# A folded, two-step DFT with a hand-given PE order, in place of a three-level DFT with PE transposes

## Chip, cores, metric

One core of one Trainium2 chip. The metric is the device time of one execution, in microseconds (us), lower is better. A run is called slow here when it took over 1.5% longer than the fastest run of the same kernel. PE is the matmul engine, DVE the vector engine, ACT the scalar engine, POOL the GpSimd engine, SP the sync engine, which in these kernels only issues DMAs.

## The reference, cut

A GFNet block followed by a token MLP, forward and backward in one program: S = 2048 tokens, D = 448, F = 1792, bf16.

```python
def _A_ref(x, w_r, w_i):                        # spectral filter
    X = rfft2(x.astype(f32), axes=(-2, -1))     # 2048 x 225 complex
    return irfft2(X * (w_r + 1j * w_i), s=(S, D)).astype(bf16)
def _B_ref(x, w1, b1, w2, b2):                  # MLP over tokens
    u = gelu(einsum("bsd,sf->bdf", _layernorm(x), w1) + b1)
    return (einsum("bdf,fs->bds", u, w2) + b2).transpose(0, 2, 1)
h  = x + _A_ref(_layernorm(x), w_r, w_i)
h2 = h + _B_ref(_layernorm(h), w1, b1, w2, b2)
# outputs: h2 and the gradients of x, w_r, w_i, w1, b1, w2, b2 for a given grad_out
```

Names used below: `u` = w1ᵀ·LN(h), `y` = w2ᵀ·g, `dg` = w2·grad_out, `dh` = w1·du; gw1, gw2 are the weight gradients (out_4, out_6); the gradients of w_r and w_i are out_2 and out_3; W is w_r and w_i together.

## The kernel before

Every transpose is done on PE (a matmul with the identity) and evicted from PSUM. The DFT over tokens is done in three levels, with one pair of 256-wide matmuls for each of 29 blocks of 8 columns. W is loaded across all 128 partitions. DMAs go out alternately on the ACT and POOL queues; SP is idle.

```python
dma_engs = [nc.scalar, nc.gpsimd]
...
def rfft2(src, dst, before_c=None):
    for t in range(NT):                                   # DFT over columns
        for j in range(4):
            nc.tensor.transpose(tp[:, j, :], src[:, t, DBASE[j]:DBASE[j] + P], ident[:])
        evac(out=xt[:], in_=tp[:])
        for j in range(4):
            nc.tensor.matmul(pa[:], lhsT=xt[:, j, :], rhs=fd[:, j, :, :], ...)
        ...
    for kb in range(NKB):                                 # 29 blocks
        for c in range(2):
            nc.tensor.transpose(tps[:, c, :], at[:, c, kb, :, :], ident[:])
        evac(out=tt[:], in_=tps[:])
        nc.tensor.matmul(pb[:], lhsT=tt[:, 0, :], rhs=kA[:], start=True, stop=False)
        nc.tensor.matmul(pb[:], lhsT=tt[:, 1, :], rhs=kB[:], start=False, stop=True)
        ...
...
dma(w_b[:, :, 0, 0:DF], A_w_r.rearrange("(q r) k -> q r k", r=NR))      # W: 128 partitions
...
def w2T_blocks(j):                                        # w2 transposed on PE for dg
    for tg in range(0, NT, 4):
        pt, _ = transpose_blocks(None, [w2t[:, j, t * P:(t + 1) * P] for t in range(tg, tg + 4)], None, "tr")
        evac(out=blk[:, tg:tg + 4, :], in_=pt[:])
```

The stages run one after the other: forward spectral, u, gw2, y, dg, gw1, dh, backward spectral.

## Time and profile before

584.12 us median of 3 runs (583.54 to 585.63). Lines of the page: busy time of PE; PE's busy share in 40 equal slices of the span, in tenths; the same for the DMA engines (mean of 16); packets; and per DMA queue its packets, megabytes, and the time that its packets took as a share of 16 engines over the span.

```profile
span 582.7 us, 8976 instructions
...
PE 472.2 (81%) x3364; PEld 281.9 (48%) x3364; DVE 360.2 (62%) x912; ACT 301.6 (52%) x640; POOL 47.1 (8%) x94
...
PE   0287687979997999999999989997999989487600
...
DMA  9030155359702333211660423331000470001124
...
DMA packets 25555, 65.53 MB, mean 112 GB/s; under 512 B 8376, under 2 KB 13560, under 8 KB 24872
...
q0 software_dynamic: 8176, 34.50, 15.6%
q10 hardware_dynamic: 17336, 30.47, 15.0%
...
```

PE is busy 472.2 of 582.7 us, so 110.5 us are idle: some 51 of them at the two ends and 49 in the two spectral stretches (windows below). The DMA queues together take 31% of the 16 engines: there is room.

The windows view gives, for a stretch of time, the busy us and instruction count of each engine, the granted PE clock, the DMA share and the GB/s:

```profile
...
core 0: us, PE busy (x) PEld busy (x) DVE busy (x) ACT busy (x) POOL busy (x), PEclk, DMA share, GB/s
0.00:28.00 28.00, 2.40 (x18) 1.67 (x18) 21.96 (x94) 8.71 (x21) 4.79 (x26) 1.00 0.48 132
28.00:129.00 101.00, 79.33 (x680) 54.81 (x681) 83.46 (x208) 70.06 (x133) 10.45 (x15) 0.97 0.34 129
...
236.00:279.00 43.00, 43.00 (x236) 22.52 (x235) 10.65 (x16) 0.76 (x2) 4.34 (x8) 1.00 0.14 53
...
458.00:558.00 100.00, 73.09 (x592) 47.85 (x590) 79.66 (x181) 62.37 (x167) 6.36 (x11) 0.91 0.22 73
558.00:583.00 25.00, 0.00 (x0) 0.00 (x0) 13.39 (x24) 0.00 (x0) 3.02 (x4) 0.50 0.40 81
...
```

236–279 (a part of the MLP) is pure PE. In the spectral stretches 28–129 and 458–558 PE is busy 79 and 73 us of about 100 and DVE 80 to 83. The ends, 0–28 and 558–583, hold 2.4 us of PE work together.

Groups of instructions (count, busy us, mean ns of one, then the engine's idle time before them and who ended it):

```profile
...
L658 ACT COPY w2T<-ps_tr 128x512 bf16<-128x512 bf16 x33 | 17.4, 592 | 73.9 <-PE ps_tr L547 52.4
L715 PE MATMUL ps_mm<-du_t,hlt 128*128 128x512 bf16 (+1 forms) x256 | 49.5, 353 | 0.3
...
L668 PE MATMUL ps_mm<-xn,w2T 128*128 128x448 bf16 x224 | 44.7, 352 | 0.0
...
L220 PE MATMUL ps_tr<-ident,cinv 128*128 128x128 bf16 x16 | 2.1, 310 | 23.4 <-ACT cinv L213 23.4
...
```

The MLP matmuls (L715, L668) wait for nothing. The w2 transposes are evicted by ACT, in pieces of 0.59 us (L658), and by DVE; PE starts only when a table is there (L220, 23.4 us).

### The profile page before, as it was taken

The page shows a single profiled execution, that of the slowest core. Times are in us where ns is not written, and L with a number is a line of the kernel's source. Part 1 is how long each engine was busy: PE and PEld are TensorE (multiplying, and loading weights), DVE is VectorE, ACT ScalarE, POOL GpSimd, SP SyncE. Part 2 cuts the span into 40 slices and gives each one's busy share as a digit, 9 for nine tenths or more (in the row PEclk, how much of TensorE's full clock was granted, in tenths as well). Part 3 has the DMA queues.
Part 4 walks back from the last instruction along what each step waited for, and adds up shares of the span by engine and source line. Part 5 has one row for each costly group of instructions (what it writes and reads, how often), then busy time and mean ns, then how long its engine had stood idle before and what let it go on. Part 6 is the DMA issues. An engine that isn't in the chain of part 4 may idle for free.

```text
span 582.7 us, 8976 instructions
## 1 busy us (share of the span) xinstructions
PE 472.2 (81%) x3364; PEld 281.9 (48%) x3364; DVE 360.2 (62%) x912; ACT 301.6 (52%) x640; POOL 47.1 (8%) x94
## 2 busy tenths in 40 slices
PE   0287687979997999999999989997999989487600
PEld 0144475544546444555666555554666557364200
DVE  5988687795779721122444343322777857967983
ACT  0569776546997655100144164443666347378800
POOL 3000013021000000110300100000000100001111
PEclk9999899999997999999999999998999999699855
DMA  9030155359702333211660423331000470001124
GB/s 253 1 127 36 74 207 190 134 181 394 274 1 112 131 158 145 96 43 46 257 265 2 164 90 144 139 127 65 0 1 2 167 219 1 0 2 33 63 85 74
DMA packets 25555, 65.53 MB, mean 112 GB/s; under 512 B 8376, under 2 KB 13560, under 8 KB 24872
## 3 DMA queue, kind: packets, MB, share of 16 engines
q0 software_dynamic: 8176, 34.50, 15.6%
q10 hardware_dynamic: 17336, 30.47, 15.0%
q8 instruction: 26, 0.43, 0.3%
q14 instruction: 17, 0.14, 0.1%
HBM read 36.27 MB, written 28.69 MB: 111 GB/s over the span
## 4 chain that ended last, share of the span: by engine, by line
PE 59%; DVE 20%; ACT 13%; issue 5%; DMA 3%; ACTq 0%; DVEq 0%
PE ps_mm L627 8%; PE ps_mm L715 8%; PE ps_mm L668 7%; PE ps_mm L636 7%; PE ps_mm L739 7%; PE ps_tr L547 5%; PE ps_mm L345 4%; PE ps_mm L393 2%; PE ps_mm L357 2%; DVE stats_h L435 1%; ACT uf L567 1%; DVE hn L523 1%; DVE gx L818 1%; DVE ln_stats L435 1%; PE ps_mm L394 1%
## 5 line engine op out<-in xcount | busy, mean ns | idle before, releaser
L658 ACT COPY w2T<-ps_tr 128x512 bf16<-128x512 bf16 x33 | 17.4, 592 | 73.9 <-PE ps_tr L547 52.4
L715 PE MATMUL ps_mm<-du_t,hlt 128*128 128x512 bf16 (+1 forms) x256 | 49.5, 353 | 0.3
L627 PE MATMUL ps_mm<-goT,g_t 128*128 128x512 bf16 x224 | 49.3, 379 | 0.0
L564 PE MATMUL ps_mm<-hln,w1c 128*128 128x448 bf16 x224 | 44.6, 362 | 3.8 <-DVE hln L442 3.8
L739 PE MATMUL ps_mm<-gp,w1T 128*128 128x448 bf16 x224 | 46.3, 361 | 0.3 <-issue 0.3
L668 PE MATMUL ps_mm<-xn,w2T 128*128 128x448 bf16 x224 | 44.7, 352 | 0.0
L636 PE MATMUL ps_mm<-gT,w2t 128*128 128x448 bf16 x224 | 42.5, 352 | 0.0
L715 PEld LDWEIGHTS <-hlt 128*128 128x128 bf16 x256 | 24.6, 98 | 24.4 <-ACT hlt L709 1.2
L564 PEld LDWEIGHTS <-w1c 128*128 128x128 bf16 x224 | 22.4, 100 | 25.8 <-issue 6.6
L627 PEld LDWEIGHTS <-g_t 128*128 128x128 bf16 x224 | 21.7, 98 | 25.3
L636 PEld LDWEIGHTS <-w2t 128*128 128x128 bf16 x224 | 21.9, 98 | 20.5
L739 PEld LDWEIGHTS <-w1T 128*128 128x128 bf16 x224 | 21.7, 100 | 19.3 <-issue 2.3
L345 PE MATMUL ps_mm<-fd,xt 128*128 128x464 bf16 x128 | 27.5, 365 | 3.8 <-DVE xt L342 3.5
L668 PEld LDWEIGHTS <-w2T 128*128 128x128 bf16 x224 | 21.4, 98 | 18.0
L670 DVE TENSOR_TENSOR gp<-ps_mm,gp 128x448 bf16<-128x448 f32 x14 | 8.7, 625 | 31.3 <-PE ps_mm L668 31.3
L357 PE MATMUL ps_mm<-kA,tt 128*128 128x256 bf16 x58 | 15.2, 278 | 7.8 <-DVE tt L355 4.5
L220 PE MATMUL ps_tr<-ident,cinv 128*128 128x128 bf16 x16 | 2.1, 310 | 23.4 <-ACT cinv L213 23.4
L743 ACT ACTIVATE junk<-ps_mm 128x448 bf16<-128x448 f32 x16 | 8.7, 544 | 22.6 <-PE ps_mm L739 22.6
L381 ACT CAST vt_t<-ps_mm 128x464 bf16<-128x464 f32 x26 | 13.1, 577 | 13.8 <-issue 8.5
L345 PEld LDWEIGHTS <-xt 128*128 128x128 bf16 x128 | 11.7, 99 | 16.4 <-DVE xt L342 4.5
L729 ACT COPY w1T<-ps_tr 128x512 bf16<-128x512 bf16 (+1 forms) x32 | 16.8, 582 | 3.0 <-DMA out_dram<-st_4501 2.9
L547 PE MATMUL ps_tr<-ident,w1n 128*128 128x128 bf16 x224 | 15.3, 219 | 3.2 <-DVE w1T L729 3.2
(676 smaller groups left out, 1112.2 us busy)
## 6 DMA issues: line engine op xcount, KB each, us to landing
w1c<-in_B_w_dram POOLq DMA_DIRECT2D x7, 1024.0 KB, 10.0
w2t<-in_B_w_dram ACTq DMA_DIRECT2D x7, 512.0 KB, 15.7
w2t<-in_B_w_dram POOLq DMA_DIRECT2D x7, 512.0 KB, 10.6
w1n<-in_B_w_dram ACTq DMA_DIRECT2D x8, 448.0 KB, 15.9
w1n<-in_B_w_dram POOLq DMA_DIRECT2D x8, 448.0 KB, 9.0
xspec_d<-xspec POOLq DMA_DIRECT2D x1, 1856.0 KB, 6.0
xspec_b<-xspec_d POOLq DMA_DIRECT2D x1, 1856.0 KB, 11.9
xln_d<-xln ACTq DMA_DIRECT2D x1, 1792.0 KB
```

The source lines that it names most:

```text
L345: nc.tensor.matmul(pa[:], lhsT=xt[:, j, :], rhs=fd[:, j, :, :], start=(j == 0), stop=(j == 3))
L357: nc.tensor.matmul(pb[:], lhsT=tt[:, 0, :], rhs=kA[:], start=True, stop=False)
L381: evac(out=vt[:, :, :, r, :], in_=pv[:, :, :].rearrange("p c (kb k) -> p c kb k", k=8))
L547: nc.tensor.transpose(pt[:, i, :], src_blocks[i], ident[:])
L564: nc.tensor.matmul(pu[:], lhsT=w1c[:, t, jj * P:(jj + 1) * P], rhs=hln[:, t, :], start=(t == 0), stop=(t == NT - 1))
L627: nc.tensor.matmul(pw[:], lhsT=g_t[:, jj, j * P:(j + 1) * P], rhs=goT[:, jj, ch * 512:(ch + 1) * 512], start=(jj == 0), stop=(jj == 3))
L636: nc.tensor.matmul(py2[:], lhsT=w2t[:, j, t * P:(t + 1) * P], rhs=gT[:, j, :], start=(j == 0), stop=(j == NFB - 1))
L658: evac(out=blk[:, tg:tg + 4, :], in_=pt[:])
L668: nc.tensor.matmul(pdg[:], lhsT=cur[:, t, :], rhs=go[:, t, :], start=(t == 0), stop=(t == NT - 1))
L715: nc.tensor.matmul(pw[:, 0:cw], lhsT=hlt[:, jj, :], rhs=du_t[:, jj, ch * 512:ch * 512 + cw], start=(jj == 0), stop=(jj == 3))
L729: evac(out=blk[:, jg:jg + n, :], in_=pt[:, 0:n, :])
L739: nc.tensor.matmul(pdh[:], lhsT=cur[:, j, :], rhs=duT[:, j, :], start=(j == 0), stop=(j == NFB - 1))
```

## The change

Intent: fewer and larger matmuls for the DFT, no transposes on PE, and no idle PE in the spectral stages, by putting matmuls of dg, gw2 and gw1 between their steps.

- The rows are folded (x[k] ± x[-k]), so the column DFT needs half the products; the token DFT has two steps, with a scatter through SBUF-to-SBUF DMAs between them.
- All transposes become DMA transposes on the SP queue.
- `fill(n)` puts n pending MLP matmuls into the PE order at given places; the other engines' orders are worked out by a timeline simulation when the kernel is built.
- In the new spectral layout, W loads and stores come in 18 pieces of 16 partitions each, on the POOL queue.

```diff
+N_FILL_F = (50, 4, 16, 3, 16, 2)
+N_FILL_B = (16, 16, 60, 9, 16, 12)
...
-        for tg in range(0, NT, 4):
-            pt, _ = transpose_blocks(None, [w2t[:, j, t * P:(t + 1) * P] for t in range(tg, tg + 4)], None, "tr")
-            evac(out=blk[:, tg:tg + 4, :], in_=pt[:])
+    def load_w2T(j):
+        wT = w2T_ring.next()
+        nc.sync.dma_start_transpose(out=wT, in_=B_w2[j * P:(j + 1) * P, :].rearrange("f (t c) -> f t c", c=P))
+        return wT
...
-    dma(w_t[:, :, 0, 0:DF], A_w_r.rearrange("(q r) k -> q r k", r=NR))
+    def w_io(Wv, dr, di, store, eng):
+            for f in range(4):
+                go((16 * f, 16 * f + 16), 0, 16,
+                   d.rearrange("(a r) k -> a r k", r=P)[:, 16 * f:16 * f + 16, :])
+            for f in range(4):
+                ...                                  # the mirrored half, again 16 partitions each
...
+    def fold_prep(src, t2):
+        ...
+        nc.sync.dma_start_transpose(out=xT, in_=ft.rearrange("p s b c -> p (s b) c"))
+    def d_stage(xT, i):                              # column DFT, then s1_stage and its scatter
+    def s1_stage(s1, ab):
+        ...
+        nc.sync.dma_start(out=D2[s1:P:16, :, 0:2, :], in_=cs)
...
+    pending.append(dg_gen())
+    w_io(W_view_F, A_w_r, A_w_i, False, gp_)
+    fill(N_FILL_F[0])                                # 50 dg matmuls ahead of the first d_stage
+    for s1 in range(NT):
+        nab = d_stage(xTs[s1 // 2], s1 % 2)
+        if s1 >= 1:
+            s1_stage(s1 - 1, ab)
+        fill(N_FILL_F[1])
...
+    nc.sync.dma_start_transpose(out=du_t.rearrange("p j b q -> p (j b) q"), in_=rD[:, 0:NFB * 4 * P])
+    w_io(W_view_B, A_w_r, A_w_i, False, gp_)
+    pending.append(gw2_gen())                        # each block of g and LN(h) through a DMA transpose
+    pending.append(gw1_gen())
+    fill(N_FILL_B[0])
...
```

## The prediction

> **What bounds it now.** The page's busy table gives PE 472 of 582.7 us, 3364 matmuls. By stage (the windows view), the three token-MLP stretches run PE-bound (190 to 334 us is nearly all PE), but the spectral ones do not: 0–28 us has 2.4 us of PE (tables; PE's largest wait is 23 us on the table `cinv`), 28–129 and 458–558 have 79 and 73 us of PE in about 100 each, with DVE at about 80%, and 558–583 has none. Spectral work with start and tail is thus about 255 us; the MLP 330, of which 30 are PE transposes of w1 and w2.
>
> **Removed.** All PE transposes and their PSUM evictions (0.59 us on ACT, 0.42 on DVE for 128x512); the three-level DFT with 29 blocks per direction (256-wide matmuls, evictions of 0.37–0.42 us); the large table chain (2048-wide ACT steps at 2 us); the serial weight-gradient tail.
>
> **Kept.** 1376 MLP matmuls. In the chain of waits 224 of width 448 take 42.4 us (189 ns each), 215 of width 512 take 46.4 (216 ns). Estimate: 266 us.
>
> **Added.** A folded DFT, per direction 64 matmuls of width 226, 80 of 452, 64 of 128, 64 of 448: at 0.1, 0.2, 0.1, 0.2 us (weight loads are 98 ns) about 42 us, so 83 for both. PE falls from 472 to about 350 (1920 matmuls).
>
> **Moved.** dg = w2ᵀ·go (224 matmuls) now fills the forward spectral stages; both weight gradients (480 matmuls, 96 us) fill the backward ones. All transposes go to DMA on the one SP queue: w2 and w1 (7.3 MB each), the folded rows, g, hln, du, go: about 26 MB. [...], mostly hidden.
>
> **Sum (estimate).** PE start at 12–15 us; forward spectral with dg 42+45 plus 15 of latency and table waits → 115; u 46, y 44; dh with six d-pairs 52; backward 96+35 → about 390; tail 8. Stalls that I expect: w1 and w2 column loads (1 MB took 10 us to land, and there are only two buffers against 6.4 us of matmuls): 10–15; w1ᵀ transposes, 448 KB per 2.8 us of PE: 10; the 1.8 MB du transpose ahead of others on SP: 10; ACT in the backward stage (120 evictions of 0.59 plus spectral ones, near 100% of it): 10. About 445 us, PE about 80% busy again.
>
> **Predicted: 445 us, 80% range 405 to 500. Faster by over 2%: 0.97; within 2%: 0.02; slower: 0.01.**
>
> **What would show it.** PE busy 345–380 us, about 1920 matmuls; no transposes on PE; PE starting before 16 us; forward spectral plus dg ending near 115 us; backward spectral plus both gradients about 140 us with PE over 85%; no long stretch without PE at the end (under 12 us); PE's remaining waits naming DMA-fed tiles (rE, r3, r2, rS) and ACT evictions, not DVE.
>
> **What would make it wrong.** DMA transposes much slower than 200 GB/s, or a head-of-line block on SP, where a transpose waits for its buffer ahead of a spectral scatter: then dg, dh or the start of the backward stage stretch by tens of us, towards 500 or more. A granted clock below the 0.945 of now[...].

The sum came to about 390 us, a tail of 8 and 40 to 45 of stalls, about 445; transposes stand in the sum only as 20 us of stalls (w1ᵀ 10, du 10). The 0.1 and 0.2 us for a matmul of the folded DFT are estimates, beside 189 and 216 ns for widths 448 and 512 and 98 ns for a weight load in the kernel before; the 200 GB/s no run had shown.

## The result

552.80 us median of 4 runs (546.42 to 558.94) against 584.64 (583.54 to 585.63) of the kernel before on the same chip: ratio 0.938, 95% interval 0.934 to 0.943, so 6% faster; correct. Predicted were 445 us, 405 to 500. A ratio is the mean time of one kernel's fast runs over that of the other's of the same rounds, so not quite the ratio of the medians that are quoted. The profile below is of the 558.94 us run, a slow one; the fast runs took 546.42 and 550.49.

```profile
span 556.8 us, 6068 instructions
...
PE 386.8 (69%) x1920; PEld 192.2 (35%) x1920; DVE 259.5 (47%) x710; ACT 232.8 (42%) x477; POOL 119.1 (21%) x177
...
PE   0135287485739888986779999935449998399990
...
DMA  9999979759956665259963999799995798986552
...
DMA packets 137344, 87.89 MB, mean 158 GB/s; under 512 B 111136, under 2 KB 127584, under 8 KB 137184
...
q1 hardware_dynamic: 125248, 43.41, 48.2%
q0 software_dynamic: 11488, 42.26, 33.4%
...
```

PE's work fell by 85 us (472.2 to 386.8, 3364 matmuls to 1920), but its idle time rose from 110 to 170 us. The DMA row went from 2 nines in 40 slices to 19: the queues now take 83% of the 16 engines, not 31%. Packets went from 25,555 to 137,344, of which 111,136 are under 512 bytes; q1 is SP's queue, with all transposes; q0 is POOL's.

Windows of after: the start; dg's first 50 matmuls; u; y; dh; and the start of the backward stage.

```profile
...
0.00:25.00 25.00, 0.00 (x0) 0.00 (x0) 16.01 (x60) 2.86 (x3) 14.19 (x29) 1.00 1.00 173
25.00:66.00 41.00, 15.97 (x50) 6.21 (x51) 14.98 (x79) 9.19 (x14) 8.99 (x17) 0.68 1.25 104
...
187.00:237.00 50.00, 43.42 (x227) 21.63 (x225) 34.54 (x90) 23.78 (x32) 6.33 (x6) 1.00 0.49 159
237.00:304.00 67.00, 51.52 (x229) 24.19 (x228) 19.23 (x39) 12.60 (x34) 15.35 (x22) 0.87 0.77 167
304.00:356.00 52.00, 50.21 (x284) 27.33 (x283) 38.99 (x114) 20.44 (x57) 1.08 (x2) 1.00 0.94 176
356.00:420.00 64.00, 32.14 (x122) 13.57 (x120) 5.06 (x15) 17.83 (x34) 13.32 (x25) 0.72 1.12 129
...
```

u and dh went about as planned (50 and 52 us against 46 and 52, clock 1.00). In 0–66 us PE did 16 us of work, with the DMA engines at 1.00 and 1.25 of their time for 173 and 104 GB/s; in 356–420 it did 32 us of 64, DMA at 1.12 for 129 GB/s. (A share over 1 says that records of packets of one engine overlap; I read it as "full".)

```profile
...
L567 PE MATMUL ps_mm<-rC,rE 128*128 128x448 bf16 x224 | 62.9, 418 | 50.0 <-DMA rE<-in_B_w_dram 50.0
L865 PE MATMUL ps_mm<-rG,rst 112*128 112x512 bf16 x224 | 59.7, 418 | 23.4 <-DMA rst<-rE 12.9
L732 PE MATMUL ps_mm<-rE,rS 128*128 128x448 bf16 x224 | 51.0, 396 | 15.5 <-DMA rS<-in_B_w_dram 15.5
...
L809 PE MATMUL ps_mm<-rD,r_73 128*128 128x448 bf16 x224 | 43.5, 353 | 0.6 <-DMA r_73<-in_B_w_dram 0.6
...
```

dg waits 50.0 us for transposed w2 (rE), 25.3 of them at the start; gw2 waits 23.4 for transposed g and for its store buffers, y 15.5 for its w2 columns (rS). dh, fed by w1 transposes of nearly the same size, waits only 0.6: in its stage POOL's queue moves 0.12 MB, against 8.96 on SP's (lines under all_plain), so almost nothing runs beside them. What SP did in the first 64 us (start, us, line, tile, count):

```profile
...
0.75 37.80 SPq L187 DMA_TRANSPOSE rE<-in_B_w_dram  x3
38.67 8.90 SPq L437 DMA_TRANSPOSE rT<-rF  x2
...
```

Three w2 transposes of 512 KB held SP for 37.8 us; the first transposes of folded rows (L437), which the spectral stage needs, stand behind them.

### The profile page after: what moved, and what is told of

Read it like the earlier page. It is cut to its first block, busy times and chain, and to the rows that moved or that the text cites. A ratio compares the mean times of both kernels' runs of the same rounds, so it can differ in the third digit from the quotient of the medians.

```text
span 556.8 us, 6068 instructions
## 1 busy us (share of the span) xinstructions
PE 386.8 (69%) x1920; PEld 192.2 (35%) x1920; DVE 259.5 (47%) x710; ACT 232.8 (42%) x477; POOL 119.1 (21%) x177
## 2 busy tenths in 40 slices
DMA packets 137344, 87.89 MB, mean 158 GB/s; under 512 B 111136, under 2 KB 127584, under 8 KB 137184
## 3 DMA queue, kind: packets, MB, share of 16 engines
q1 hardware_dynamic: 125248, 43.41, 48.2%
q0 software_dynamic: 11488, 42.26, 33.4%
## 4 chain that ended last, share of the span: by engine, by line
DMA 41%; PE 21%; issue 14%; DVE 10%; POOL 7%; ACT 4%; SPq 2%; DVEq 0%; POOLq 0%; ACTq 0%
PE ps_mm L809 6%; PE ps_mm L732 5%; DMA rS<-in_B_w_dram 5%; DMA out_dram<-r_81 4%; DMA rG<-in_A_w_r_dram 4%; DMA r_72<-in_B_w_dram 4%; DMA rD<-in_A_w_i_dram 4%; DMA r_73<-r_78 3%; DMA rE<-in_B_w_dram 3%; DMA rC<-rD 3%; PE ps_mm L880 3%; PE ps_mm L865 2%; DMA xspec_d<-rS 2%; DMA rD<-in_A_w_r_dram 2%; DMA out_dram<-rO 2%
## 5 line engine op out<-in xcount | busy, mean ns | idle before, releaser
L567 PE MATMUL ps_mm<-rC,rE 128*128 128x448 bf16 x224 | 62.9, 418 | 50.0 <-DMA rE<-in_B_w_dram 50.0
L865 PE MATMUL ps_mm<-rG,rst 112*128 112x512 bf16 x224 | 59.7, 418 | 23.4 <-DMA rst<-rE 12.9
L732 PE MATMUL ps_mm<-rE,rS 128*128 128x448 bf16 x224 | 51.0, 396 | 15.5 <-DMA rS<-in_B_w_dram 15.5
L880 PE MATMUL ps_mm<-rC,rst 112*128 112x512 bf16 (+1 forms) x256 | 54.9, 363 | 3.3 <-ACT rO L883 2.0
L567 PEld LDWEIGHTS <-rE 128*128 128x128 bf16 x224 | 24.5, 113 | 78.5 <-DMA rE<-in_B_w_dram 51.6
L687 PE MATMUL ps_mm<-rB,r_72 128*128 128x448 bf16 x224 | 43.5, 353 | 6.6 <-DMA r_72<-in_B_w_dram 4.4
L809 PE MATMUL ps_mm<-rD,r_73 128*128 128x448 bf16 x224 | 43.5, 353 | 0.6 <-DMA r_73<-in_B_w_dram 0.6
L868 ACT CAST rO<-ps_mm 128x512 bf16<-128x512 f32 x54 | 30.4, 598 | 29.7 <-DMA out_dram<-rO 20.5
L865 PEld LDWEIGHTS <-rst 112*128 112x128 bf16 x224 | 23.6, 106 | 55.0 <-issue 20.9
L880 PEld LDWEIGHTS <-rst 112*128 112x128 bf16 x256 | 24.8, 100 | 26.2 <-issue 4.1
L528 PE MATMUL ps_ff<-csI,rAT 113*128 113x448 bf16 x128 | 31.2, 369 | 0.8 <-ACT rAT L517 0.5
L687 PEld LDWEIGHTS <-r_72 128*128 128x128 bf16 x224 | 21.6, 98 | 28.3 <-DMA r_72<-in_B_w_dram 5.9
L517 ACT CAST rAT<-ps_ff 113x512 bf16<-113x512 f32 x32 | 18.6, 589 | 30.2 <-PE ps_ff L514 30.2
L739 DVE SCALAR_TENSOR_TENSOR r_81<-ps_mm,b2col,r_81 128x448 bf16<-128x448 f32 x16 | 10.6, 681 | 43.9 <-DMA r_81<-h_d 37.3
L744 ACT ACTIVATE r_81<-rC 128x448 bf16<-128x448 bf16 x16 | 9.2, 576 | 51.9 <-DVE r_81 L739 38.9
L450 ACT CAST r_78<-ps_ff 128x452 bf16<-128x452 f32 x32 | 17.1, 539 | 30.7 <-PE ps_ff L447 30.5
L809 PEld LDWEIGHTS <-r_73 128*128 128x128 bf16 x224 | 21.7, 97 | 22.9 <-issue 1.8
L463 DVE TENSOR_SCALAR r_72<-r_72 128x904 bf16<-128x904 bf16 x8 | 2.7, 391 | 48.5 <-DMA r_72<-r_78 48.5
```

The costliest lines, as they stand in the source:

```text
L450: sc.copy(out=ab, in_=pv)
L517: sc.copy(out=aT[0:KC].rearrange("p a b -> p (a b)"), in_=pa[0:KC, :])
L528: nc.tensor.matmul(py[:, 0:D], lhsT=aT[0:KC, i, :], rhs=csI[0:KC, i // 2, i % 2, :], start=(i == 0), stop=(i == 3))
L567: nc.tensor.matmul(pg[:, 0:D], lhsT=wT[:, t, :], rhs=go_tp[:, t, :], start=(t == 0), stop=(t == NT - 1))
L687: nc.tensor.matmul(pu[:, 0:D], lhsT=w1c[:, t, jj * P:(jj + 1) * P], rhs=hln[:, t, :, :], start=(t == 0), stop=(t == NT - 1))
L732: nc.tensor.matmul(py[:, 0:D], lhsT=w2cs[t // 2][:, j, (t % 2) * P:(t % 2 + 1) * P], rhs=g_[:, j, :, :], start=(j == 0), stop=(j == NFB - 1))
```

## The experiments

18 kernels ran, in five calls; the kernel before ran beside each call, at 584.9 to 587.0 us, so the chips agree within 0.4%. The changed kernel itself was not run again on those chips, so a gain over it is worked out from the two ratios to the kernel before, (0.938 - ratio) x 585 us, where both have a ratio. (w_wide_split's 0.895 matches the mean of its three runs of 522 to 528 over the kernel before's, not its one fast run of 513.) The four runs of the changed kernel, 546 to 559, show no gap between fast and slow. Kernels with the same, or nearly the same, forward direction ended it at 180.6 to 189.6 us (changed kernel, stores_on_act, y_queue, w_reload, stores_held), so less than 10 us there says nothing. The profiles of the changed kernel, w_wide, stores_on_act, staged_yfree, order_late, combined_staged and best_try are of slow runs; the changed kernel's took 8 to 13 us longer than its fast ones, so stage differences against it can hold that much more than the ratios give. "Wrong" marks a kernel that gives wrong results. The stages, in us, from PE's timeline in each profiled run ("rest" is everything after dh; sums are the span):

| kernel | median | ratio to before | first d stage at | forward end | u | y | dh | rest |
|---|---|---|---|---|---|---|---|---|
| predicted, before 40–45 of stalls | 445 | 0.762 | – | 115 | 46 | 44 | 52 | 139 |
| changed kernel | 552.8 | 0.938 | 66.4 | 187.2 | 50.0 | 66.3 | 52.2 | 201.1 |
| w_wide (wrong) | 515.9 | (one fast run) | 49.0 | 161.3 | 51.3 | 67.0 | 51.7 | 186.5 |
| w_wide_split (wrong) | 523.0 | 0.895 | 43.9 | 165.1 | 49.9 | 67.8 | 52.8 | 175.7 |
| w2_plain (wrong) | 529.2 | 0.901 | 35.3 | 156.9 | 51.7 | 71.0 | 53.0 | 197.2 |
| stores_on_act | 563.6 | (one fast run) | 63.6 | 180.6 | 49.8 | 67.2 | 53.0 | 211.6 |
| all_plain (wrong) | 505.4 | 0.863 | 31.1 | 157.3 | 48.9 | 61.2 | 51.4 | 185.7 |
| w_late | 561.3 | 0.958 | 40.1 | 188.2 | 51.4 | 72.0 | 53.3 | 198.7 |
| y_queue | 558.2 | 0.952 | 65.6 | 182.6 | 49.8 | 77.8 | 52.4 | 193.5 |
| w_reload | 530.3 | 0.908 | 64.0 | 180.7 | 51.6 | 70.6 | 53.2 | 176.9 |
| w_staged | 542.2 | 0.924 | 53.8 | 171.5 | 48.0 | 70.9 | 53.3 | 197.2 |
| staged_plain (wrong) | 488.3 | 0.833 | 30.7 | 148.5 | 50.5 | 60.0 | 51.4 | 174.3 |
| y_free | 549.5 | (two fast runs) | 62.1 | 187.6 | 48.5 | 58.0 | 53.3 | 199.4 |
| staged_yfree | 539.8 | 0.910 | 58.0 | 185.9 | 50.3 | 63.2 | 53.4 | 191.7 |
| order_late | 561.0 | 0.948 | 47.9 | 189.8 | 51.5 | 68.9 | 53.5 | 197.7 |
| stores_held | 543.4 | 0.921 | 71.5 | 189.6 | 51.2 | 67.1 | 53.1 | 181.0 |
| combined | 542.6 | 0.923 | 47.3 | 198.5 | 46.6 | 57.2 | 53.3 | 181.5 |
| combined_staged | 537.9 | 0.909 | 38.5 | 183.8 | 46.1 | 61.6 | 52.7 | 193.4 |
| folds_first | 538.1 | 0.920 | 28.1 | 163.3 | 49.8 | 71.2 | 52.1 | 199.1 |
| best_try | 513.5 | 0.870 | 26.6 | 186.1 | 47.1 | 56.7 | 51.9 | 172.2 |

### Narrow W transfers: w_wide, w_wide_split

Theory N: a transfer to 16 partitions takes long and slows what runs beside it. The rivals are that the transposes alone make the start slow (w_wide) and the number of DMAs (w_wide_split). In the changed kernel's trace the forward pieces of 112.5 KB took 19.9 us (w_r) and 11.4 us (w_i) to land (medians of seven), waits included: a piece of 7.0 KB took 12.7.

```diff
-    w_io(W_view_F, A_w_r, A_w_i, False, gp_)      # and the same for W_view_B
+    for c_, d in ((0, A_w_r), (1, A_w_i)):         # wrong order of rows, same bytes
+        gp_.dma_start(out=W_view_F[:, :, c_, 0:DF], in_=d.rearrange("(q r) k -> q r k", r=NG))
```

> The spectral weights are loaded 128 partitions wide, two transfers for each direction, in place of 18 narrow ones of 16 partitions each (same bytes and the same 450-byte pieces; rows in the wrong order, so the result is wrong on purpose). Theory N (narrow W loads hog the 16 DMA engines while others wait): the first dg group of PE starts before 20 us instead of 25, the 50-matmul fill ends near 45 instead of 66, the stall of PE between 378 and 418 us of the old trace shrinks by 20 to 25, total 495 to 510 us. Rival T (the DMA transposes themselves are too slow at the start): the fill still ends after 58 us, total above 525.

515.89 us (507.80 to 519.57), wrong. The queue lines of its page:

```profile
...
q1 hardware_dynamic: 125248, 43.41, 47.3%
q0 software_dynamic: 10720, 42.25, 30.2%
...
```

POOL's queue (q0) moved the same 42.25 MB in 30.2% of 517.8 us = 156 us of all engines, against 33.4% of 556.8 = 186 in the changed kernel: 30 us less. SP's queue, on which nothing changed, took 245 us (47.3%), not 268: so the time of a packet seems to contain waiting for other traffic, and one stream's saving shows on both. Its one fast run, 507.8, stands against 546.4 and 550.5 of the changed kernel. The d stage starts 17 us earlier, the forward direction ends 26 us earlier, the rest is 15 shorter: theory N in the main. The start itself did not move (first dg group at 27.8, was 25.4), which N had not said: the first w2 transposes are slow for another reason.

w_wide_split loads the same bytes, as wide, in 16 DMAs for each of w_r and w_i:

```diff
+    [... in_=d.rearrange("(q r) k -> q r k", r=NG)[:, g:g + 1, :] for g in range(NG)]   # one DMA per g
```

> The same bytes in 16 transfers per weight, each 128 partitions wide and one row per partition (wrong order again). If it is the narrowness of the destination that costs: as w_wide, 495 to 515 us. If it is the number of transfers (each some 0.5 us of issue on POOL and its fixed time): close to after, 535 to 552.

(In the changed kernel POOL took 0.51 to 0.60 us to issue one narrow forward W load. As for time that does not shrink with the size, its stores of 3.5, 4.0 and 7.0 KB took 2.4, 1.7 and 1.8 us to land, those of 512 KB 5.6.)

522.98 us (513.23 to 528.21), ratio to before 0.895 (0.889 to 0.901). 32 DMAs per direction, against 18 narrow ones, and still 25 us faster than the changed kernel (0.938 - 0.895); its one fast run, 513.2, is 33 to 37 under the changed kernel's. So the count is not what costs; narrowness remains. One more thing differs: the second half of the narrow pieces reads its rows backwards. In the changed kernel's forward direction the four plain pieces of w_r took 21.4 us to land (median) and the mirrored ones 14 to 20, so that is not what makes them slow; the wide pieces of w_wide_split, half as large, took 5.0. What in a narrow piece takes the time, no run shows.

### Transposes: w2_plain, all_plain

```diff
-        nc.sync.dma_start_transpose(out=wT, in_=B_w2[j * P:(j + 1) * P, :].rearrange("f (t c) -> f t c", c=P))
+        nc.sync.dma_start(out=wT, in_=B_w2[j * P:(j + 1) * P, :].rearrange("f (t c) -> f t c", c=P))   # wrong
```

> The 14 blocks of w2 for dg are loaded by plain copies instead of DMA transposes (wrong values on purpose); the narrow W loads stay. Theory T: the first three blocks land in under 20 us, the fill of 50 matmuls ends before 40 us, forward part ends 30 to 40 us earlier, total 510 to 520. Theory N: the fill still waits on W traffic and ends at 50 or later; total 535 or more.

529.15 us (524.31 to 531.62), ratio 0.901 (0.895 to 0.907). The first dg group starts at 10.3 us, not 25.4, the d stage at 35.3. The forward end comes 30 us earlier, as theory T has it, but the total, 22 us less by the ratios, lies between the two theories: y did not gain (71.0, was 66.3).

all_plain does the same to every large transpose (w2, w1, folded rows, g, LN(h), du, grad_out):

> All DMA transposes of weights, rows, g, hln and du become plain copies of about the same bytes (result wrong on purpose; W loads stay narrow). Theory T (the transposes' small packets fill the DMA engines, which everything shares): the page's packet count falls by more than half, backward loses 40 us or more, time 460 to 500. Rival C (what costs is only the order of the one SP queue, or the low granted clock, not the work of a transpose): bytes and order are the same, so the time stays within 3% of after's 546, over 530.

505.40 us (502.67 to 506.30), ratio 0.863 (0.860 to 0.867), 44 us under the changed kernel: theory T, rival C falls. Packets and queues on its page:

```profile
...
DMA packets 41984, 87.88 MB, mean 174 GB/s; under 512 B 5408, under 2 KB 25696, under 8 KB 41696
...
q1 hardware_dynamic: 29888, 43.40, 32.4%
q0 software_dynamic: 11488, 42.26, 31.0%
...
```

And the first line of SP's timeline (start, us):

```profile
...
0.75 1.34 SPq L187 DMA_DIRECT2D rE<-in_B_w_dram  x3
...
```

Same bytes and same order on q1, but the packets took 32.4% of 504.5 us = 163 us of all 16 engines, against 48.2% of 556.8 = 268. So with transposes the queue's packets take 105 us of full DMA time more. Not all of it is work: POOL's queue, on which nothing changed, also fell, from 186 to 156 us (31.0%). And the three w2 blocks that held SP for 37.8 us leave it in 1.34. The dh stage shows the cost of the transposes with almost nothing beside them. The DMA view of 304:356 us in the changed kernel, then of 267:319 in all_plain:

```profile
...
q1 hardware_dynamic: 32472, 8.96, 92.5%
q0 software_dynamic: 80, 0.12, 0.7%
...
q1 hardware_dynamic: 4248, 8.96, 56.8%
q0 software_dynamic: 128, 0.23, 1.3%
...
```

The same 8.96 MB (13 blocks of w1 and 7 of folded rows, and some scatters that are plain in both) took 48.1 us of all 16 engines with transposes and 29.5 as copies: 186 GB/s against 303. So part of the cost is the transposes' own. In this stage it is still hidden: dh takes 52.2 and 51.4 us.

The expected loss of 40 us in the backward stage was wrong: "rest" is 15 shorter, the forward end 30 earlier, y 5 shorter.

### Both together: w_staged, staged_plain

w_staged is a correct way to widen W: a permutation from DRAM to DRAM, then a load (or, for out_2 and out_3, a store) of 128 partitions.

```diff
+            go(wd[0:64, c_, :, :].rearrange("(f a) g k -> f a (g k)", a=16), bass.AP(d.tensor, d.offset, [[16 * DF, 4], [P * DF, 16], [1, 16 * DF]]))
+            ...                                                    # mirrored half, as before but into DRAM
+            eng.dma_start(out=Wv[:, :, c_, 0:DF], in_=wd[:, c_, :, :])
```

> Correct result. All narrow W transfers (forward load, backward load, and the stores of out_2 and out_3) become a permutation from DRAM to DRAM and a load or store that spans 128 partitions. Theory N (16-partition transfers are what is dear): as with the wide wrong loads, d stage at 44 to 52 us instead of 66, the gap from dh to the first backward s2 near 50 us, and the wait at the backward scatter shrinks with the narrow stores gone; time 500 to 520. Rival: what is dear is the 450-byte piece, not the narrowness; then the permutation costs the same again on the DMA engines, and the time stays at 540 or more.

542.17 us (540.70 to 549.07), ratio 0.924 (0.921 to 0.927). Between the two theories: the d stage starts at 53.8 (13 earlier), the gap from dh to the first backward s2 step shrank from 66 to 45 us as expected, but the wait at the backward scatter rose from 9.4 to 16.0 us, where out_2 and out_3 are now moved twice (a likely cause; stores_held below bears on it). By the ratios 8 us were gained.

staged_plain is w_staged with plain copies for transposes (wrong):

> Wrong result on purpose: w_staged with every large transpose a plain copy of the same bytes. If narrow W transfers and transposes together are what the prediction left out, this falls to 455 to 475, near the 445 predicted with nearly free DMA; if a third thing matters as much (granted clock, head-of-line order), it stays over 485.

488.27 us (486.51 to 490.56), ratio 0.833 (0.830 to 0.836), over the 455 to 475 that would have closed the case. By the ratios the miss is (0.938 - 0.762) x 585 = 103 us; the two DMA costs give back 61 of them, and 42 are left. The stage table shows where: forward 148.5 against 115, y 60.0 against 44, rest 174.3 against 139. In its first 150 us PE waits 12.0 us for grad_out, 18.7 in all for ACT's evictions and sign flips of the spectral chain, 6.5 for the scatter, 6.0 for w2 blocks, 5.0 for a table.

### Order of queues: stores_on_act, y_queue, y_free

stores_on_act moves the out_6 and out_4 stores from POOL to ACT.

```diff
-                            gp_.dma_start(out=out_6[j * P:(j + 1) * P, :], in_=o)      # and out_4
+                            sc.dma_start(out=out_6[j * P:(j + 1) * P, :], in_=o)
```

> The stores of both weight gradients are issued from ACT instead of POOL, so that they no longer queue behind the 18 W loads of the backward pass. Theory Q (head-of-line block on the POOL queue is what stops PE between 382 and 418 us): those waits, on the store buffers, fall from about 20 us to under 8, total 530 to 537. Theory N: the W loads saturate the DMA engines anyway and the s2 stage still waits for W or for scatters; under 8 us gained.

563.61 us (554.82 to 563.98), one fast run: no gain, rest 10 us longer. The wait moved from store buffers (10.5) to the transposes of g (12.9 to 23.2). Issued from ACT, the stores gained nothing: the 10.5 us of one wait became 10.3 more of the other. Which DMA engine ran what, this run does not show.

y_queue moves the h_d reads and the out_5 store to ACT:

```diff
-        nc.sync.dma_start(out=ht, in_=h_d[t * P:(t + 1) * P, :])
+        sc.dma_start(out=ht, in_=h_d[t * P:(t + 1) * P, :])
-    gp_.dma_start(out=out_5.rearrange("(j p) -> j p", p=P), in_=gb1r[0:NFB, :])
+    sc.dma_start(out=out_5.rearrange("(j p) -> j p", p=P), in_=gb1r[0:NFB, :])
```

> Correct result. The h_d reads and the out_5 store leave the SP and POOL queues for the ACT queue, in the y stage only. Theory Q-y (the y stage's 15 us over plan are a head-of-line block: h_d reads stand behind the grad_out transposes on SP, w2 loads behind out_5 on POOL): y falls from 66 us to 48 to 55, time down 8 to 15. Rival B (the DMA engines are full in y): y stays at 62 or more and the time within 5 us.

558.24 us (554.78 to 567.55); y is longer, 77.8: this form of the theory falls. POOL's waits in the y stage:

```profile
...
POOL out_dram L740 <- DVE r L739: 42.0, 9, 14.6
POOL rS L666 <- PE ps_mm L732: 33.0, 4, 19.9
...
```

POOL still stood 42 us before out_0 stores (L740) that wait for DVE, and the w2 column loads (L666) came behind them. So y_free moves those stores to ACT too, and takes the bias-gradient step out of the buffer ring:

```diff
-        junk = m448.next()
-        sc.activation(out=junk, in_=go_pt[:, t, :], func=ACT.Copy, accum_out=gb2[:, t:t + 1])
+        sc.activation(out=go_pt[:, t, :], in_=go_pt[:, t, :], func=ACT.Copy, accum_out=gb2[:, t:t + 1])
-        gp_.dma_start(out=out_0[0, t * P:(t + 1) * P, :], in_=h2)          # h_d and out_5 as in y_queue
+        sc.dma_start(out=out_0[0, t * P:(t + 1) * P, :], in_=h2)
```

> Correct result. In the y stage, stores and reloads of h go to the ACT queue, so that the POOL queue holds nothing but the w2 column loads, and the bias-gradient step no longer takes a buffer of the ring that the reloads need. Theory Q2 (w2 column loads stand behind stores that wait for DVE): y falls from 66 to 50 to 55 us, PE's wait on rS under 5 us, time down about 10. Rival B (the loads land late since the DMA engines are full): y over 60.

549.54 us (541.68 to 551.26). y falls to 58.0 (kernels that leave y alone and keep the transposes: 66.3 to 72.0; the five with this edit: 56.7 to 63.2), and POOL now waits only for PE to free its two buffers:

```profile
...
POOL rS L666 <- PE ps_mm L732: 51.8, 6, 19.6
```

So a part of the y stage's excess was a head-of-line block; but PE's wait for w2 columns fell only from 15.5 to 11.1 us, not under 5, and y stays over the 50 to 55 expected. The total hardly moved, and the forward row stage (from its first L528 matmul to u) shows why: it took 31.6 us instead of 22.1. Without a ring buffer to wait for, all sixteen bias-gradient steps (L744) moved up in ACT's order, between the evictions (L517) that the row stage waits for. ACT's timeline of best_try, which has the same edit:

```profile
...
169.80 0.56 ACT L744 ACTIVATE rC<-rC 128x448 bf16<-128x448 bf16 x1
...
170.91 0.56 ACT L744 ACTIVATE rC<-rC 128x448 bf16<-128x448 bf16 x1
...
171.47 0.57 ACT L517 CAST rAT<-ps_ff 113x512 bf16<-113x512 f32 x1
...
```

Each costs ACT about 0.56 us; in 154–187 us ACT is busy 24.0 us in y_free and 14.3 in the changed kernel. The 8 us gained in y were lost one stage earlier, in all five kernels with this edit (row stages of 30 to 32 us, 21 to 22 in all others). That is read from the traces; no run moved the bias steps alone. staged_yfree is this on top of w_staged:

> Correct result. w_staged and y_free together. If their gains add: 490 to 512, under both given kernels. If y_free only moves the wait: within 2% of w_staged.

539.80 us (530.93 to 546.27), ratio 0.910 (0.904 to 0.916), within 2% of w_staged.

### Where the backward stage loses: w_reload, stores_held

w_reload stores the loaded W once to DRAM, contiguous, and reloads it in one DMA for the backward direction.

```diff
+    gp_.dma_start(out=w_d[:], in_=W_view_F)
...
-    w_io(W_view_B, A_w_r, A_w_i, False, gp_)
+    gp_.dma_start(out=W_view_B, in_=w_d[:])
```

> Correct result. The backward W loads of 18 narrow pieces become one wide contiguous reload from a DRAM copy made in the forward direction. Theory N: the stretch from the end of dh to the first backward s2 shortens from 66 to 45 to 52 us, as it did with wide wrong loads, time 525 to 535. Rival: below 5 us gained, since the du transpose and the hln/g transposes hold SP there.

530.31 us (528.56 to 534.84), ratio 0.908 (0.903 to 0.913), correct. The rest falls from 201 to 177, the gap from dh to s2 from 66 to 43, a little more than N expected: 18 us by the ratios, the most that one correct edit gave.

stores_held adds a one-column DVE step that makes the out_2 and out_3 stores wait for the scatter:

```diff
+    ve.scalar_tensor_tensor(out=W_view_B[:, :, :, 0:1], in0=D3[:, :, :, 0:1], scalar=0.0, in1=W_view_B[:, :, :, 0:1], op0=ALU.mult, op1=ALU.add)
     w_io(W_view_B, out_2, out_3, True, gp_)
```

> Correct result. w_reload with the 18 narrow stores of out_2 and out_3 held until the backward scatter has landed, by one small DVE step that reads the scattered tile. Theory S (the narrow stores fill the DMA engines under the scatter): PE's wait for the backward scatter falls from 9 us to under 3, the backward stage is 6 to 10 us shorter than w_reload's 178, time 518 to 526. Rival: the scatter itself takes that long; wait and time as in w_reload (530, within 4).

543.39 us (537.57 to 552.33), ratio 0.921 (0.915 to 0.927). The first part of theory S holds: PE's wait for the backward scatter fell from 8.2 us to 1.5. But the held stores now stand on POOL before those of out_4, gw1 waits 17.3 us for its output buffers, and the rest is 4 us longer than w_reload's. The wait was moved, not taken away. (The total also has a forward end 9 us later than w_reload's, with the same forward edit.)

### Where the forward stage loses: w_late, order_late, folds_first

w_late holds the forward W loads until the first spectral result exists.

```diff
+        if s1 == 1:
+            ve.tensor_copy(out=W_view_F[:, :, :, 0:1], in_=ab[:, 0, 0:32].rearrange(...)); w_io(W_view_F, A_w_r, A_w_i, False, gp_)
```

> Correct result. The 18 narrow W loads of the forward direction are held until the first spectral result exists, so nothing narrow shares the DMA engines with the first w2 transposes. Theory N (narrow loads delay them): first dg group at 18 to 20 us instead of 25, d stage at 35 to 48 instead of 66; part is lost again where W is needed later (POOL issues them between its table expansions); time 520 to 540. Rival X (the transposes' own packets beside the x and grad_out loads set the start): first dg still at 24 to 27 us, d stage over 55, time over 540.

561.32 us (558.87 to 565.55). First dg at 28.2: rival X, the narrow loads do not set the start. The d stage starts at 40.1, earlier than rival X has it, but the forward end is 188.2, as before: PE's wait for w2 before dg fell from 50.0 to 28.2 us, and its wait for folded rows rose from 3.8 to 28.7.

order_late puts no dg ahead of the first spectral stage:

```diff
-N_FILL_F = (50, 4, 16, 3, 16, 2)
+N_FILL_F = (0, 2, 32, 5, 32, 4)
```

> Correct result. Only the PE order of the forward stages changes: no dg matmul stands ahead of the first spectral stage (50 in the changed kernel), two after each of its steps, the rest later. Theory O (the late start is the order: PE stands at dg waiting for w2 transposes while folded rows are ready): the d stage starts at 30 to 45 us instead of 66, the forward direction ends 10 to 25 us earlier, time 525 to 540. Rival D (the DMA engines set it: fold transposes stand behind the w2 transposes anyway): d stage still over 55 or slow in itself, forward end within 6 us of 187, time over 543.

560.95 us (553.46 to 564.23). The d stage starts at 47.9 and the forward direction ends at 189.8: the PE order alone is worth nothing, so theory O falls in this form. SP shows what was left in the way:

```profile
...
0.75 37.84 SPq L187 DMA_TRANSPOSE rE<-in_B_w_dram  x3
38.71 5.09 SPq L437 DMA_TRANSPOSE rT<-rF  x2
...
```

The folded rows were still behind three w2 transposes, until 38.7 us. folds_first makes those wait for the last folded block:

```diff
+        wT = w2T_ring.next(); j > 2 or ve.tensor_copy(out=wT[:, 0, 0:1], in_=fts[1][:, 0, 0, 0:1])
-N_FILL_F = (50, 4, 16, 3, 16, 2)
+N_FILL_F = (0, 0, 48, 6, 32, 4)
```

> Correct result. The changed kernel with the w2 transposes kept off the queue and off the DMA engines until the last folded row block is transposed (a one-column write makes them wait), and no dg matmul before the first spectral stage is done. In order_late three w2 transposes still stood first and held the SP queue until 38.7 us. Theory T (w2 transposes, first in line, delay x, the folds and so the start): d stage starts at 22 to 32 us and the forward direction ends at 160 to 175 instead of 187; time 525 to 540. Rival: the w2 transposes' engine time comes back later in full (dg waits for them from 60 us on): forward end within 6 us of 187, time over 543.

538.14 us (533.73 to 541.58), ratio 0.920 (0.915 to 0.924), correct. The d stage starts at 28.1 and the forward direction ends at 163.3, both as theory T has it. By the ratios 11 us are gained, not 24: y took 5 us longer, and the changed kernel's profile is a slow one.

```profile
...
22.03 5.95 SPq L437 DMA_TRANSPOSE rT<-rF  x3
...
53.09 5.20 SPq L187 DMA_TRANSPOSE rE<-in_B_w_dram  x2
...
```

Folds now come at 22 us, and two w2 transposes at 53 us hold SP for 5.2 us together, not 12.6 each.

### Sums: combined, combined_staged, best_try

combined is w_reload, stores_held, y_free and order_late; combined_staged also stages the forward W.

> Correct result. w_reload, held stores, the freed y stage and the later dg order together. If the gains add: 490 to 510. If they overlap (the DMA engines stay full and waits move): 515 to 530.

542.55 us (538.40 to 564.37): no sum of gains. It carries two edits that give back what they gain (the held stores, the early bias steps), and order_late, in which the transposes still stand in the way.

> Correct result. As combined, but the forward W too comes through a DRAM to DRAM permutation and a wide load. If narrow W transfers still matter in the forward direction: 5 to 15 us under combined. If the later dg order already hides them: within 4 us.

537.86 us (530.16 to 540.25), ratio 0.909 against 0.923: 8 us under combined, within what was expected for narrow W.

best_try has folds_first, the staged forward W, the contiguous reload and the freed y stage:

> Correct result. folds_first, forward W through a DRAM to DRAM permutation and a wide load, backward W as one contiguous reload, and the freed y stage; stores of out_2 and out_3 as in the changed kernel. If the parts add: forward end at 145 to 160 us, y 58 to 62, backward 165 to 180, time 495 to 515. If the DMA engines' work is the bound and only moves: 525 to 540, as combined.

513.48 us median of 6 (505.87 to 535.45), ratio to before 0.870 (0.866 to 0.873), correct: the fastest correct version, 13% under the kernel before and 7% under the changed kernel (0.870 over 0.938). y (56.7) and rest (172.2) came in, or under, what was expected. The forward end, 186.1 against 163.3 in folds_first, did not: the row stage took 30 us with the bias steps in it (21), the dg matmuls waited 16.5 us for w2 (10.7), and the matmuls at L502 13.5 us for ACT (5.5). What lies behind the last two no run shows. Lines of its page:

```profile
span 514.0 us, 6045 instructions
...
PE 380.8 (74%) x1920; PEld 192.4 (37%) x1920; DVE 261.2 (51%) x712; ACT 227.6 (44%) x474; POOL 103.5 (20%) x146
...
```

Putting the bias steps back behind the row stage, or the forward W loads narrow as in folds_first, was not run.

## Why the prediction was wrong

**The direction and the PE side were right.** Faster by over 2% was given 0.97. Matmuls are 1920 as said; no PE transposes are left; u took 50 us (46), dh 52 (52). PE's busy time is 387 us, a little over 345–380. The longest waits named are DMA-fed tiles, as expected.

**The step that failed: the 26 MB of transposes as "mostly hidden".** Two things in it failed.

- *The size.* The time put on the stream rested on a rate that no run had shown, and on that alone. What the runs show: with almost nothing beside them (dh stage), transposes with some scatters got 186 GB/s: at that rate 26 MB take 140 us, an estimate. Over the whole kernel they got less: SP's queue took 268 us of all 16 engines, and 163 with the same bytes copied plainly (all_plain). The plain rate there is 43.4 MB in 163 us, so 26 MB would take 98; adding the 105 us gives about 203 us for 26 MB, some 130 GB/s. This too is an estimate, from the profile pages of those two runs, and waiting for other traffic is in it. By these estimates the stream takes all 16 engines for 140 us by itself and for some 60 more in this traffic; the sum held 20 us of stalls for it.
- *"Mostly hidden."* It set the stream against the whole span, but the w2 transposes were put where all else is being loaded. There three of them held SP for 37.8 us (1.34 as copies), the folds stood behind them, and PE did 16 us of work in 66. Moving them out of the way (folds_first) brought the forward end from 187 to 163.

**Left out: the W loads.** The sum has no term for them, though the diff shows 18 narrow DMAs in place of 2 wide ones in each direction. Made wide (wrongly) they give back 25 us (w_wide_split, by its ratio) to about 40 (the one fast run of w_wide); a correct reload in the backward direction alone gives 18.

**Mis-sized: the spectral chain and y.** With both DMA costs cut (staged_plain) the forward direction still takes 148 us, not 115 (against "15 of latency and table waits" the waits named above are 48), y 60, not 44, and the rest 174, not 139. These excesses (33, 16 and 35 us, with 5 in u) are partly covered by the 40 to 45 us of stalls in the sum; 42 us are not. For y a part is shown: w2 column loads behind stores that wait, 8 us (y_free, 58); what stays is mostly the wait for w2 columns with two buffers (11.1 us), which the prediction had among its stalls. For the rest of these 42 us the cause stays open; the waits point to grad_out and to the many short dependent steps from ACT.

**Of "what would make it wrong"**, the first condition came true in both parts: transposes under 200 GB/s (186 in the dh stage), and a head-of-line block on SP, though at the start it came from transposes that were slow (37.8 us for three), not from one that waited for its buffer. But it was given as a tail risk with "500 or more", outside the range. The other, "A granted clock below the 0.945 of now", came true in number (0.876 to 0.895 in the four runs), but not where PE is dense: the clock was 1.00 in the u and dh stages (PE busy 43.4 of 50 and 50.2 of 52 us), 0.68 in 25–66 us and 0.72 in 356–420, where PE waited (16.0 of 41 and 32.1 of 64). (The 1.00 of 0–25 us says nothing: the trace holds no clock record before 29.6 us, and the view counts that as 1.00.) So in these stages a low clock goes with waits; which of the two brings the other was not shown, since no run changed the clock alone.

**Of the signs:** PE started at 25 us, not before 16; the forward part ended at 187, not near 115; the backward part ran at 70% PE (32.1 + 54.6 + 53.7 of 201 us), not over 85%; the end without PE is 14 us (542.3 to 556.8), not under 12, but less than the 25 of before.

## What to carry to other kernels

A transpose moved from PE to DMA is not free because PE does not see it (here the transposes cost the program 44 us, all_plain): count its time on the 16 DMA engines and on the queue that issues it, add every other transfer of that stage, and ask what stands behind it on the same queue (here the folded rows, behind three transposes that held SP for 37.8 us). Price each stage's DMA against that stage, not against the span, and look at the partition count of every transfer that a new layout brings (W in pieces of 16 partitions, not 128, cost 25 us or more, w_wide_split). When an edit takes a wait away, look at where the freed instruction goes: a scheduler may put it in front of something that matters (the row stage of y_free, 31.6 us instead of 22.1).
